# Linear attention and a SwiGLU block on one core: the statements from the eleventh chunk of tile 0 on in another order, some casts, multiplications and additions on another engine

## The chip, the core and the metric

The kernel runs on one core of a Trainium2 chip. A core has five engines with a queue each: TensorE (PE in the profile; its weight loads are PEld), VectorE (DVE), ScalarE (ACT), GpSimd (POOL) and SyncE (SP), which here issues nearly all transfers. An engine executes its queue in order; engines wait for each other by semaphores. 16 DMA engines move the data between device memory (HBM) and the on-chip memory, and one kind of transfer, the DMA transpose, also transposes. TensorE multiplies: it loads a block of weights, streams a second operand past it, and writes into one of eight accumulation banks. The metric is device time in microseconds (us) of one execution, the median of several.

## The reference: what is computed

Attention without softmax, with a decay `lam` for each head, in blocks of 64 positions, and a SwiGLU block on its result. q, k and v are 4 x 8 x 768 x 64 (batch, head, position, dimension), x is 3072 x 512, the weights are 512 x 1536 (two) and 1536 x 512.

```python
for b in range(nb):
    sl = slice(b * block, (b + 1) * block)
    qb, kb, vb = (q[:, :, sl].copy(), k[:, :, sl].copy(), v[:, :, sl].copy())
    intra = np.einsum('bhic,bhjc->bhij', qb, kb) * Dmask[None]
    intra = np.einsum('bhij,bhjd->bhid', intra, vb)
    inter = np.einsum('bhid,bhde->bhie', qb * lam_pow[None], kv_state)
    out[:, :, sl] = intra + inter
    ...
    kv_state = lam_block[None, :, None, None] * kv_state + np.einsum('bhsd,bhse->bhde', kb_dec, vb)
...
x = np.ascontiguousarray(attn_out.transpose(0, 2, 1, 3)).reshape(B * S, H * D)
g = x @ w_gate
silu = g * (1.0 / (1.0 + np.exp(-g)))
val = x @ w_val
return (silu * val @ w_out).astype(np.float32)
```

## The kernel before

The work is cut into twelve groups of the attention (256 positions of one batch element each, all heads) and six tiles of the SwiGLU block (512 tokens each, two groups). Group g feeds tile g // 2, so the attention of the next groups runs between the matmuls of the tile at hand. Everything is written out by hand: the kernel has a manual schedule, and each engine's queue holds its instructions in the order in which the statements stand. `use(...)` names the accumulation banks that the next statement takes.

For a group g the statements are:

- `load_fp32(g, ...)`: k, q and v from HBM, on SyncE's queue
- `kcast(g)` (ScalarE) and `qcast(g, engine)`: k rounded to bf16, q multiplied by its decay and rounded, both into the tile `qk`; `v_scale(g, engine)`: v times its decay, into `v_s`
- `dma_transpose(g)`: `qk` transposed into `qkt`, a DMA on SyncE's queue (L268), from group 3 on; groups 0 to 2 are transposed on TensorE
- `scores(g)`: k times q on TensorE (reads `qkt`); `mask(g, ...)`: the causal mask, on VectorE
- `upd_mm(g)`: this group's contribution to the state (reads `qk` and `v_s`); `sadd`, `kvn`, `kvm`, `kv0c`, `kvz`, `kvf0`: additions to the running state, its decay, and casts of it to bf16
- `op_new(g)` / `op_bare(g)`, `inter(g, first)`, `intra(g, first)`: the output, from the state (reads `qkt`) and from the masked scores; between the two stands `guard(g)`, a ScalarE copy of one column of the bank, for which the second of them waits
- `evr(g, r, engine)`: the output out of the bank, as the tile `xt` of the SwiGLU block

For a tile t: `ffn_gate(t, fc, b0, b1)` and `ffn_val(t, fc, b0, b1)` are 4 matmuls each for one chunk fc (128 of 1536 hidden features) and blocks b0 to b1 of the tile's tokens; the first ends in the SiLU on ScalarE (tile `sil`, four buffers), the second in the multiplication of `sil` by the bank on VectorE (into `h`). `ffn_out(t, b)` is the last product for 128 tokens of tile 0. Tiles 1 to 5 have their last product, and tiles 4 and 5 the first two as well, in a form with seven products of quarter size and sums of the operands (`hs_new`, `hsum`, `oprod`, `w_combo`, `x_combo`, `unit`, `uprod`, `silu`, `mu`, `mup`, `wo_combo`). The weights arrive in pieces (`w_piece`, `wo_piece`) and are rounded by `w_cast` and `wo_cast`. All loads but one pair at the start, the transposes and the stores but one stand in SyncE's queue. q, k, raw weights and several of the sums share ten buffers.

The lines that matter below: `inter(2, False)` L992, `evr(2, 0, DVEC)` L993, `kcast(3)` L996, `qcast(3, nc.gpsimd)` L997, `dma_transpose(3)` L998, the loads after it from L999 on, `v_scale(3, nc.gpsimd)` L1002, `dma_transpose(4)` L1019, `load_fp32(5, nc.sync, v, "v")` L1020, the six `wo_piece` from L1021 on, `scores(3)` L1035, `dma_transpose(5)` L1072, `inter(4)` L1098 and `upd_mm(5)` L1103, `ffn_out(0, 0)` L1119, `ffn_gate(2, 3, 0, 2)` L1122, `inter(5)` L1124, `scores(5)` L1125.

Of the kernel before, what the change touches and what calls it, by code (L numbers as in the profile page):

```python
# [37 lines left out]
def _body(ctx, tc, nc, q, k, v, lam, moe_w_gate, moe_w_val, moe_w_out, out):  # L38
# [896 lines left out]
    def use(*bk):  # L935
        fixed[:] = bk
# [72 lines left out]
    use(0); ffn_gate(1, 0, 0, 2)  # L1009
    use(1); ffn_val(1, 0, 0, 2)  # L1010
    use(2); ffn_gate(1, 1, 0, 2)
    use(3); ffn_val(1, 1, 0, 2)
    use(4); ffn_gate(1, 2, 0, 2)
    use(5); ffn_val(1, 2, 0, 2)
    use(6); ffn_gate(1, 3, 0, 2)
    use(7); ffn_val(1, 3, 0, 2)
    kcast(4)
    qcast(4, nc.vector)
    dma_transpose(4)  # L1019
# [7 lines left out]
    use(0); ffn_gate(1, 4, 0, 2)  # L1027
    use(1); ffn_val(1, 4, 0, 2)
    use(2); ffn_gate(1, 5, 0, 2)
    use(3); ffn_val(1, 5, 0, 2)  # L1030
    use(4); ffn_gate(1, 6, 0, 2)
    use(5); ffn_val(1, 6, 0, 2)
    use(6); ffn_gate(1, 7, 0, 2)
    use(7); ffn_val(1, 7, 0, 2)
    use(0, 1, 2, 3); scores(3)  # L1035
    use(4, 5); upd_mm(3)
    mask(3, 1, 0)
    mask(3, 0, 0)
    mask(3, 0, 1)
# [3 lines left out]
    use(7); ffn_val(1, 8, 0, 2)  # L1043
    mask(3, 1, 1)
    use(2); ffn_gate(1, 9, 0, 2)
    use(4); ffn_gate(1, 10, 0, 2)
    use(6); ffn_val(1, 9, 0, 2)
    use(0, 1); op_new(3)
    inter(3, True)
    use(2); ffn_val(1, 10, 0, 2)  # L1050
    guard(3)
    intra(3, False)
    use(3, 4); upd_mm(4)
    evr(3, 0, DVEC)
    kcast(5)
    evr(3, 1, ACTC)
    use(7); ffn_gate(1, 11, 0, 2)
    sadd(3, 1)
    sadd(4, 0)
    use(2); ffn_val(1, 11, 0, 2)  # L1060
    kvn(4, 0, ACTC)
    use(6); ffn_gate(1, 0, 2, 4)
    use(1); ffn_gate(1, 1, 2, 4)
    use(0); ffn_gate(1, 2, 2, 4)
    sadd(4, 1)
    qcast(5, nc.vector)
    use(5); ffn_gate(1, 3, 2, 4)
    use(2); ffn_val(1, 1, 2, 4)
    use(7); ffn_val(1, 2, 2, 4)
    use(6); ffn_val(1, 0, 2, 4)  # L1070
    use(1); ffn_gate(1, 4, 2, 4)
# [4 lines left out]
    use(3); ffn_gate(1, 5, 2, 4)  # L1076
    use(2, 0, 6, 4); scores(4)
    v_scale(5, nc.gpsimd)
    kvm(3, nc.gpsimd)
# [4 lines left out]
    mask(4, 0, 1)  # L1084
    mask(4, 1, 1)
    use(3); ffn_val(1, 3, 2, 4)
    mask(4, 1, 0)
    use(5); ffn_gate(1, 6, 2, 4)
    use(7); ffn_val(1, 4, 2, 4)
    use(4); ffn_gate(1, 7, 2, 4)  # L1090
    use(3); ffn_val(1, 5, 2, 4)
    use(1); ffn_gate(1, 8, 2, 4)
    use(7, 4); op_new(4)
    use(0); ffn_gate(1, 9, 2, 4)
    use(6); ffn_val(1, 9, 2, 4)
    mask(4, 0, 0)
    use(3); ffn_val(1, 6, 2, 4)
    inter(4, True)  # L1098
    guard(4)
    w_combo(0, 0, (0, 3))  # L1100
    use(6); ffn_val(1, 7, 2, 4)
    intra(4, False)
    use(3, 5); upd_mm(5)  # L1103
    evr(4, 1, ACTC)
    evr(4, 0, ACTC)
    new_xt(3)
    use(1); ffn_gate(1, 10, 2, 4)
    use(0); ffn_val(1, 8, 2, 4)
    use(4); ffn_gate(1, 11, 2, 4)
    use(7); ffn_gate(2, 0, 0, 2)  # L1110
    use(0); ffn_val(2, 0, 0, 2)
    wo_cast(ACTC)
    use(2); ffn_gate(2, 1, 0, 2)
    wo_combo(0)
    sadd(5, 0)
    use(1); ffn_val(1, 10, 2, 4)
    wo_cast()
    kvn(5, 0, ACTC)
    use(4); ffn_out(0, 0)  # L1119
    use(0); ffn_val(1, 11, 2, 4)  # L1120
    use(7); ffn_gate(2, 2, 0, 2)
    use(4); ffn_gate(2, 3, 0, 2)  # L1122
    use(1, 6); op_new(5)
    inter(5, True)  # L1124
    use(3, 2, 7, 0); scores(5)  # L1125
    kvm(4, nc.vector)
    mask(5, 1, 0)
    mask(5, 0, 0)
    mask(5, 0, 1)
    w_combo(1, 0, (0, 3))  # L1130
    sadd(5, 1)
    wo_combo(1)
    mask(5, 1, 1)
    guard(5)
    kcast(6)
    use(4); ffn_out(0, 1)
    qcast(6, nc.vector)
    dma_transpose(6)
# [4 lines left out]
    use(7); ffn_out(0, 2)  # L1143
    intra(5, False)
    evr(5, 0, ACTC)
    evr(5, 1, ACTC)
    hs_new(1)
    use(2); ffn_out(0, 3)
    hsum(1, 0, 0, 6, 0, 1)
    hsum(1, 0, 0, 6, 1, 2)  # L1150
    hsum(1, 1, 0, 6, 1, 2)
    wo_combo(2)
    hsum(1, 2, 0, 6, 0, 1)
    use(7); ffn_gate(2, 0, 2, 4)
    use(5); ffn_val(2, 1, 0, 2)
    use(0); ffn_val(2, 3, 0, 2)
    use(6); ffn_val(2, 2, 0, 2)
    use(4); ffn_val(2, 0, 2, 4)
    hsum(1, 1, 0, 6, 0, 1)
    use(5); ffn_gate(2, 1, 2, 4)  # L1160
    hsum(1, 2, 0, 6, 1, 2)
    wo_combo(3)
    v_scale(6, nc.vector)
    use(7); ffn_gate(2, 2, 2, 4)
    use(2); ffn_gate(2, 3, 2, 4)
    use(3); ffn_val(2, 2, 2, 4)
    hsum(1, 3, 0, 6, 0, 1)
    use(7); ffn_val(2, 1, 2, 4)
    use(0); ffn_gate(2, 4, 0, 4)
    use(5); ffn_val(2, 4, 0, 4)  # L1170
    use(1); ffn_gate(2, 5, 0, 4)
    kcast(7)
    use(3, 4); scores(6)
    use(6, 2); upd_mm(6)
    mask(6, 0, 1)
    use(7); ffn_val(2, 5, 0, 4)
    sadd(6, 0)
    kvm(5, nc.gpsimd)
    qcast(7, nc.gpsimd)
# [4 lines left out]
    out_new(1, (0,), [0, 1, 7], 0)  # L1184
    oprod(1, 0, 1)
    kvn(6, 0, ACTC)
    w_combo(0, 1, (0, 3))
    use(4); ffn_val(2, 3, 2, 4)
    sadd(6, 1)
    use(5); ffn_gate(2, 6, 0, 4)  # L1190
    oprod(1, 0, 7)
    oprod(1, 0, 2)
    kvn(6, 1, ACTC)
    v_scale(7, nc.vector)
    sadd(6, 2)
    mask(6, 0, 0)
    kv0c(3, ACTC)
    use(4); ffn_gate(2, 7, 0, 4)
    kvn(6, 2, ACTC)
    oprod(1, 0, 6)  # L1200
    sadd(6, 3)
    use(6); ffn_val(2, 6, 0, 4)
    hsum(1, 3, 0, 6, 1, 2)
    oprod(1, 0, 5)
    oprod(1, 0, 4)
    use(0); ffn_val(2, 7, 0, 4)
# [3 lines left out]
    use(3, 7); op_new(6)  # L1210
    inter(6, True)
    use(0, 4); upd_mm(7)
    use(2, 6); scores(7)
    kvm(6, nc.vector)
    sadd(7, 0)
    v_scale(8, nc.gpsimd, 0, 4)
    guard(6)
    kvn(7, 0, ACTC)
    mask(7, 0, 0)
    sadd(7, 1)  # L1220
    intra(6, False)
    evr(6, 1, ACTC)
    use(1); ffn_gate(2, 8, 0, 4)
    kvn(7, 1, ACTC)
    kcast(8)
    sadd(7, 2)
    mask(7, 0, 1)
    use(5); ffn_val(2, 8, 0, 4)
# [5 lines left out]
    out_new(1, (1,), [2, 1, 7], 0)  # L1234
    oprod(1, 1, 7)
    oprod(1, 1, 1)
    use(6); ffn_gate(2, 9, 0, 4)
    kvn(7, 2, ACTC)
    sadd(7, 3)
    oprod(1, 1, 6)  # L1240
    v_scale(8, nc.vector, 4, 8)
    w_combo(1, 1, (0, 3))
    use(0); ffn_gate(2, 10, 0, 4)
    evr(6, 0, ACTC)
    use(5); ffn_val(2, 10, 0, 4)
    use(6); ffn_val(2, 9, 0, 4)
    oprod(1, 1, 4)
    oprod(1, 1, 2)
    oprod(1, 1, 5)
    hs_new(2)  # L1250
    use(7, 3); op_new(7)
    inter(7, True)
# [431 lines left out]
```

## Time and profile before

| | |
|---|---|
| time, median of 3 | 216.13 us (216.01 to 216.83) |
| the profiled execution's own time | 215.75 us |
| its span, first to last instruction | 214.0 us |
| granted TensorE clock | 1.00 |
| TensorE busy | 207.5 us, 97% of the span, 2801 matmuls |
| VectorE, ScalarE, GpSimd busy | 157.5, 131.8, 50.9 us |
| moved by DMA | 39.77 MB, mean 186 GB/s |
| q, 512 KB a load, median from issue to landing | 7.5 us |
| w_out, 512 KB a piece, median from issue to landing | 9.1 us |
| DMA transpose, median from issue to landing | 3.9 us |

How to read it: the page is one profiled execution. Lines of a timeline give start and length in us, engine, line of the kernel, operation, output <- input, sizes, and how often; in brackets stands how long the engine was idle just before, and what ended that. The busy rows of the page cut the span into 40 slices of 5.35 us; each digit is a busy share in tenths. Matmuls overlap each other, so how far apart they start says more than how long each is; their ends are modelled. For SyncE (SPq) the length of a line is the time in which it issues the transfer, not that of the transfer. A transfer lands in 16 parts, one for each DMA engine, and the trace records each.

### The profile page before, as it was taken

The page shows a single profiled execution, that of the slowest core. Times are in us where ns is not written, and L with a number is a line of the kernel's source. Part 1 is how long each engine was busy: PE and PEld are TensorE (multiplying, and loading weights), DVE is VectorE, ACT ScalarE, POOL GpSimd, SP SyncE. Part 2 cuts the span into 40 slices and gives each one's busy share as a digit, 9 for nine tenths or more (in the row PEclk, how much of TensorE's full clock was granted, in tenths as well). Part 3 has the DMA queues.
Part 4 walks back from the last instruction along what each step waited for, and adds up shares of the span by engine and source line. Part 5 has one row for each costly group of instructions (what it writes and reads, how often), then busy time and mean ns, then how long its engine had stood idle before and what let it go on. Part 6 is the DMA issues. An engine that isn't in the chain of part 4 may idle for free.

```text
span 214.0 us, 6802 instructions
## 1 busy us (share of the span) xinstructions
PE 207.5 (97%) x2801; PEld 153.0 (72%) x2801; DVE 157.5 (74%) x302; ACT 131.8 (62%) x283; POOL 50.9 (24%) x72
## 2 busy tenths in 40 slices
PE   7799999999999999999999999999999999999993
PEld 3466455888886558767654545888888888888883
DVE  1673447679774798889779899999887589982851
ACT  6788576657446443667677385946873677536522
POOL 6585755704472010300101030040200000000200
PEclk9999999999999999999999999999999999999999
DMA  6999999999996697989677869776000500005014
GB/s 187 343 352 373 378 365 324 266 256 222 356 335 132 168 280 188 240 204 261 156 189 163 208 144 248 185 69 228 6 3 3 196 0 3 0 0 199 0 54 147
DMA packets 82177, 39.77 MB, mean 186 GB/s; under 512 B 45410, under 2 KB 77794, under 8 KB 82146
## 3 DMA queue, kind: packets, MB, share of 16 engines
q1 hardware_dynamic: 80946, 38.74, 66.7%
q10 hardware_dynamic: 1200, 0.59, 1.0%
q8 instruction: 22, 0.36, 0.7%
q14 instruction: 9, 0.07, 0.1%
HBM read 28.31 MB, written 6.29 MB: 162 GB/s over the span
## 4 chain that ended last, share of the span: by engine, by line
PE 92%; SPq 3%; DMA 2%; POOL 1%; issue 0%; ACT 0%; DVE 0%
PE bank L814 22%; PE bank L600 20%; PE bank L618 20%; PE bank L755 17%; PE bank L638 5%; SPq L109 2%; DMA v<-in_v_dram 2%; PE bank L541 2%; PE bank L554 2%; PE bank L408 1%; PE bank L347 1%; POOL v_s L260 1%; PE bank L383 1%; PE bank L310 0%; ACT kvf L501 0%
## 5 line engine op out<-in xcount | busy, mean ns | idle before, releaser
L622 DVE TENSOR_TENSOR h<-sil,bank 128x256 bf16<-128x256 bf16 (+1 forms) x67 | 35.0, 532 | 21.4 <-PE bank L618 17.2
L618 PE MATMUL bank<-xt,wv_sb 128*128 128x256 bf16 (+1 forms) x276 | 50.2, 314 | 0.0
L600 PE MATMUL bank<-xt,wg_sb 128*128 128x256 bf16 (+1 forms) x276 | 50.1, 315 | 0.0
L605 ACT ACTIVATE sil<-bank 128x256 bf16<-128x256 f32 (+1 forms) x67 | 31.6, 477 | 22.3 <-PE bank L600 15.7
L618 PEld LDWEIGHTS <-wv_sb 128*128 128x128 bf16 x276 | 26.6, 98 | 14.7
L600 PEld LDWEIGHTS <-wg_sb 128*128 128x128 bf16 x276 | 26.1, 98 | 12.9
L260 POOL TENSOR_TENSOR v_s<-v,dec 128x512 bf16<-128x512 f32 (+1 forms) x15 | 18.6, 1254 | 60.9 <-DMA v<-in_v_dram 19.8
L814 PEld LDWEIGHTS <-h 128*128 128x128 bf16 x240 | 23.5, 98 | 3.6
L814 PE MATMUL bank<-wo_sb,h 128*128 128x256 bf16 x180 | 22.3, 273 | 0.0
L814 PEld LDWEIGHTS <-hs 128*128 128x128 bf16 x180 | 17.5, 98 | 3.4 <-DVE hs L673 0.2
L362 DVE TENSOR_TENSOR ssb<-bank,causal 128x512 bf16<-128x512 f32 x24 | 15.5, 684 | 3.6 <-PE bank L347 3.5
L814 PE MATMUL bank<-wt,hs 128*128 128x256 bf16 x120 | 15.6, 272 | 0.0
L755 PEld LDWEIGHTS <-ws 128*128 128x128 bf16 x144 | 14.0, 98 | 1.8
L755 PE MATMUL bank<-xs,ws 128*128 128x256 bf16 x96 | 13.9, 272 | 0.0
L763 DVE TENSOR_TENSOR bank<-bank,es 128x512 f32<-128x512 f32 x12 | 8.3, 697 | 7.2 <-PE bank L755 4.4
L780 DVE TENSOR_TENSOR h<-sil,bank 128x512 bf16<-128x512 bf16 x18 | 11.8, 679 | 1.5 <-ACT sil L774 1.2
L780 POOL TENSOR_TENSOR h<-sil,es 128x512 bf16<-128x512 bf16 x1 | 1.2, 1162 | 46.7 <-DVE es L765 46.7
L774 ACT ACTIVATE sil<-bank 128x512 bf16<-128x512 f32 x18 | 10.2, 593 | 2.1 <-PE bank L755 2.1
L638 PE MATMUL bank<-wo_sb,h 128*128 128x512 bf16 x48 | 10.9, 379 | 0.0
L755 PE MATMUL bank<-xt,wv_sb 128*128 128x256 bf16 x72 | 10.8, 273 | 0.0
L443 ACT CAST kvn<-kvf 64x256 bf16<-64x256 f32 x22 | 8.9, 403 | 3.1 <-DVE kvf L489 2.7
L278 ACT CAST qk<-kraw 128x1024 bf16<-128x1024 f32 x9 | 9.4, 1042 | 1.8 <-DMA kraw<-in_k_dram 1.8
(127 smaller groups left out, 342.9 us busy)
## 6 DMA issues: line engine op xcount, KB each, us to landing
out_dram<-osb SPq DMA_DIRECT2D x22, 256.0 KB, 2.7
v<-in_v_dram SPq DMA_DIRECT2D x18, 256.0 KB, 4.3
woraw<-in_moe_w_out_dram SPq DMA_DIRECT2D x6, 512.0 KB, 9.1
kraw<-in_k_dram SPq DMA_DIRECT2D x24, 128.0 KB, 3.2
qraw<-in_q_dram SPq DMA_DIRECT2D x24, 128.0 KB, 3.8
wraw<-in_moe_w_gate_dram SPq DMA_DIRECT2D x5, 512.0 KB, 6.9
wraw<-in_moe_w_val_dram SPq DMA_DIRECT2D x5, 512.0 KB, 6.7
kraw<-in_k_dram SPq DMA_DIRECT2D x4, 512.0 KB, 6.3
```

Source lines behind the costliest of these rows:

```text
L260: eng.tensor_tensor(out=st[("vs", g)][:, h0:h1], in0=st[("v", g)][:, h0:h1].rearrange("p h (s d) -> p h s d", s=2), in1=vfac(g, h0, h1), o ...
L278: fn(out=qk_new(g)[:, 0].rearrange("p s (h d) -> p h s d", h=H), in_=st[("kraw", g)].rearrange("p h (s d) -> p h s d", s=2))
L362: nc.vector.tensor_tensor(out=st[("ssb", g)][:, h2, 2 * c:2 * c + 2].rearrange("p a s n -> p a (s n)"), in0=st[("sp", g, c, h2)].rearrange ...
L600: nc.tensor.matmul(gp[:, n0:n1], wg_sb[:, mc, fs], xt[:, g0:g1, mc].rearrange("p g b n -> p g (b n)"), start=(mc == 0 and n0 == 0), stop=( ...
L605: nc.scalar.activation(sil[:, 0:N], gp[:, 0:N], AF.Silu)
L618: nc.tensor.matmul(vp[:, n0:n1], wv_sb[:, mc, fs], xt[:, g0:g1, mc].rearrange("p g b n -> p g (b n)"), start=(mc == 0 and n0 == 0), stop=( ...
L622: nc.vector.tensor_tensor(out=h_sb[:, fc % FH, b0:b1].rearrange("p b n -> p (b n)"), in0=sil[:, 0:N], in1=vp[:, 0:N], op=ALU.mult)
L638: nc.tensor.matmul(ps, st[("h", t, fc // FH)][:, fc % FH, b], wo_sb[:, fc, c0:c1], start=(fc == 0), stop=(fc == FC - 1))
L755: nc.tensor.matmul(o[i][:, fi * 256:fi * 256 + 256], lhs(c, 2 * j + fi), rhs(c), start=(k < 2 and fi == 0 and c == 0), stop=(c == KH - 1), ...
L774: nc.scalar.activation(sil[half, r], unit_src(t, j, half, r)[0], AF.Silu)
L780: eng.tensor_tensor(out=st[("h", t, half)][:, 2 * j:2 * j + 2][:, :, r:B:2], in0=v3(st[("u", t, j)][4][half, r]), in1=v3(unit_src(t, j, ha ...
L814: nc.tensor.matmul(o, lhs(f), rhs(f), start=(k in (1, 7) and f == 0), stop=(f == FH - 1), skip_group_check=True)
```

## The change

Up to chunk 9 of tile 0 (counted from 0) and `scores(2)` the kernels are equal. From there to the end the same statements, with the same shapes, stand in another order, and many take other accumulation banks. The functions are unchanged; no work is added or left out. The order on SyncE's queue is the same.

On another engine stand: `v_scale(3)` and `qcast(3)` (GpSimd before, VectorE after), `kvm(3)` and `kvm(5)` (GpSimd, then VectorE), `kv0c(2)` (GpSimd, then ScalarE), the second half of `v_scale(8)` (VectorE, then GpSimd), `mup(4, 0)` (VectorE, then GpSimd) and `evr(10, 1)` (VectorE, then ScalarE). The one-line pieces of `hsum`, `mask`, `sadd`, `kvn`, `silu` and `mu` move with the rest.

The beginning of the diff, with all that concerns groups 2 and 3:

```diff
     use(2, 3, 4, 5); scores(2)
+    use(6); ffn_gate(0, 10, 0, 4)
     mask(2, 0, 0)
+    mask(2, 1, 0)
     mask(2, 0, 1)
-    mask(2, 1, 0)
     mask(2, 1, 1)
-    use(6); ffn_gate(0, 10, 0, 4)
-    use(7); ffn_val(0, 10, 0, 4)
     use(0); ffn_gate(0, 11, 0, 2)
-    use(1); ffn_val(0, 11, 0, 2)
-    use(2, 3); upd_mm(2)
+    use(2); ffn_gate(0, 11, 2, 4)
+    use(1); ffn_val(0, 10, 0, 4)
+    use(7, 2); upd_mm(2)
+    use(6, 0); op_bare(2)
+    intra(2, True)
+    kcast(3, ACTC)
     kvz(2)
-    kvf0(2)
-    use(4, 5); op_bare(2)
-    intra(2, True)
     guard(2)
     inter(2, False)
     evr(2, 0, DVEC)
+    use(4); ffn_val(0, 11, 2, 4)
+    use(6); ffn_val(0, 11, 0, 2)
+    v_scale(3, nc.vector)
+    qcast(3, nc.vector)
     evr(2, 1, ACTC)
-    sadd(2, 1)
-    kcast(3)
-    qcast(3, nc.gpsimd)
+    use(3); ffn_gate(1, 0, 0, 2)
+    use(1); ffn_gate(1, 1, 0, 2)
     dma_transpose(3)
     load_fp32(4, nc.sync, v, "v")
-    use(6); ffn_gate(0, 11, 2, 4)
-    use(7); ffn_val(0, 11, 2, 4)
-    v_scale(3, nc.gpsimd)
-    v_scale(4, nc.gpsimd)
-    kvm(2, nc.gpsimd)
-    kv0c(2, POOLC)
     load_fp32(5, nc.sync, k, "kraw")
     load_fp32(5, nc.sync, q, "qraw")
...
+    use(2); ffn_gate(1, 7, 0, 2)
+    use(7, 1, 0, 3); scores(3)
...
+    use(0, 3); op_new(4)
+    inter(4, True)
+    use(6, 7); upd_mm(5)
+    guard(4)
+    intra(4, False)
...
+    use(3); ffn_gate(2, 1, 0, 2)
+    use(4); ffn_gate(2, 2, 0, 2)
+    use(1); ffn_out(0, 0)
+    kv0c(2, ACTC)
+    use(5, 0); op_new(5)
+    use(2, 6, 4, 3); scores(5)
+    inter(5, True)
...
+    use(2); ffn_val(2, 2, 0, 2)
     qcast(6, nc.vector)
+    use(3); ffn_gate(2, 3, 0, 2)
```

In the new order `ffn_val(1, 7, 0, 2)` stands after `scores(3)` and `upd_mm(4)`, and `ffn_gate(2, 3, 0, 2)` after `scores(5)` and `inter(5)`; both stood ahead of them before.

More of the change, by code (lines that the diff above doesn't have):

```diff
@@ L1075, in _body @@
     load_fp32(6, nc.sync, v, "v")
[L1076 to L1079, printed above, removed]
+    mask(4, 1, 1)
+    mask(4, 1, 0)
+    use(3); ffn_gate(1, 8, 2, 4)
+    use(1); ffn_val(1, 4, 2, 4)
+    use(5); ffn_val(1, 8, 2, 4)
+    use(4); ffn_val(1, 6, 2, 4)
+    use(0, 3); op_new(4)
[3 more added lines that the diff above has]
+    intra(4, False)
+    w_combo(0, 0, (0, 3))
+    new_xt(3)
+    evr(4, 0, ACTC)
+    use(1); ffn_gate(1, 9, 2, 4)
+    evr(4, 1, ACTC)
+    use(5); ffn_gate(1, 10, 2, 4)
+    use(4); ffn_val(1, 7, 2, 4)
+    use(0); ffn_val(1, 10, 2, 4)
+    use(2); ffn_gate(1, 11, 2, 4)
     wo_cast()
@@ L1209, in _body @@
     store(1, 0, 0, 0, 512, None)
-    use(3, 7); op_new(6)
+    use(5, 6); op_new(6)
     inter(6, True)
-    use(0, 4); upd_mm(7)
-    use(2, 6); scores(7)
-    kvm(6, nc.vector)
+    use(4, 1); upd_mm(7)
+    use(0, 3); scores(7)
     sadd(7, 0)
-    v_scale(8, nc.gpsimd, 0, 4)
     guard(6)
     kvn(7, 0, ACTC)
-    mask(7, 0, 0)
[L1220 to L1224, printed above, removed]
+    intra(6, False)
+    sadd(7, 1)
+    v_scale(8, nc.gpsimd, 0, 4)
+    kvn(7, 1, ACTC)
+    kv0c(4, ACTC)
+    use(7); ffn_gate(2, 8, 0, 4)
+    use(2); ffn_gate(2, 9, 0, 4)
+    kv0c(3, ACTC)
+    v_scale(8, nc.gpsimd, 4, 8)
+    mask(7, 0, 1)
+    mask(7, 0, 0)
+    kvm(6, nc.vector)
+    sadd(7, 2)
     kcast(8)
-    sadd(7, 2)
-    mask(7, 0, 1)
-    use(5); ffn_val(2, 8, 0, 4)
+    w_combo(1, 1, (0, 3))
     qcast(8, nc.vector)
@@ L1418, in _body @@
     uprod(4, 0, 6, 0)
-    silu(4, 0, 1, 0)
-    use(3, 5); op_new(10)
-    hs_new(4)
+    use(2, 3); upd_mm(11)
     inter(10, True)
-    use(7, 0); upd_mm(11)
     uprod(4, 0, 6, 1)
     sadd(11, 0)
+    silu(4, 0, 1, 1)
+    silu(4, 0, 1, 0)
     silu(4, 0, 0, 1)
```

690 lines of the change are left out of this document (332 added, 358 removed).

## The prediction

> **What bounds the kernel now.** I read the page first: the busy shares, then the slices.
>
> ```profile
> span 214.0 us, 6802 instructions
> ...
> PE 207.5 (97%) x2801; PEld 153.0 (72%) x2801; DVE 157.5 (74%) x302; ACT 131.8 (62%) x283; POOL 50.9 (24%) x72
> ...
> PE   7799999999999999999999999999999999999993
> ...
> PEclk9999999999999999999999999999999999999999
> DMA  6999999999996697989677869776000500005014
> ```
>
> PE is busy throughout but for the first two slices and the last, at full clock, and DMA is saturated in the first third. A busy PE can hide waits, so I looked at how far apart matmuls start: 109 ns for 256 columns and 216 ns for 512, almost everywhere after 16 us. What is lost there is small: 0.49 us at 38.1 us (inter(2) after the guard), and after 70 us five gaps of 0.05 to 0.11 us, 0.41 us in all. Each change of tile size costs 0.093 us going into a group of 64x64 matmuls and about 0.12 us coming out. So reordering has little to win, about 1 us, and can only lose by making PE wait for something that comes late. Therefore I looked for what PE waits for already: the weight loads, then SyncE's queue.
>
> ```profile
> 70.29 0.11 PEld L541 LDWEIGHTS <-kv 64*64 64x64 bf16 x2 [0.21 <-DMA qkt<-qk]
> ```
>
> This is inter(5), at its first weight load: PE gets there in the same tenth of a microsecond as the transposed k and q of group 5. It is the only place after 16 us where PE depends on a transfer with no margin. The queue that brings it:
>
> ```profile
> 36.08 1.35 SPq L109 DMA_DIRECT2D qraw<-in_q_dram  x1
> 40.73 2.33 SPq L268 DMA_TRANSPOSE qkt<-qk  x1
> 43.11 0.57 SPq L109 DMA_DIRECT2D v<-in_v_dram  x1
> 43.72 0.58 SPq L109 DMA_DIRECT2D kraw<-in_k_dram  x1
> 44.34 1.46 SPq L109 DMA_DIRECT2D qraw<-in_q_dram  x1
> 45.97 5.44 SPq L268 DMA_TRANSPOSE qkt<-qk  x1
> 51.45 0.58 SPq L109 DMA_DIRECT2D v<-in_v_dram  x1
> 52.09 3.89 SPq L249 DMA_DIRECT2D woraw<-in_moe_w_out_dram  x6
> 56.14 10.39 SPq L268 DMA_TRANSPOSE qkt<-qk  x1
> 66.58 3.51 SPq L124 DMA_DIRECT2D kraw<-in_k_dram  x4
> ```
>
> The transposes are those of groups 3, 4 and 5 (start, then length). SyncE holds its queue while it issues one (2.33, 5.44, 10.39 us: the later two until what is ahead has nearly landed). From 36.08 to 40.73 it waits for the casts that the first transpose reads; after that nothing pauses for over a microsecond until 66.5, and the DMA share of the stretches is 0.8 to 1.3 (0.45 in 41 to 42 us). What is late at 40.73 is late at 70.17, where the last of the 16 parts of transpose 5 lands.
>
> **The change, part by part.** SyncE's instructions stand in the same order in both programs. What decides when transpose 3 starts is this:
>
> ```profile
> 39.60 1.04 ACT L278 CAST qk<-kraw 128x1024 bf16<-128x1024 f32 x1
> 37.73 1.91 POOL L282 TENSOR_TENSOR qk<-qraw,dec 128x1024 bf16<-128x1024 f32 x1 [1.70 <-DVE ssb L362]
> 39.60 1.91 POOL L260 TENSOR_TENSOR v_s<-v,dec 128x1024 bf16<-128x1024 f32 x1
> 38.44 0.73 DVE L569 CAST xt<-bank 128x512 bf16<-128x512 f32 x1
> ```
>
> Before: qcast(3) ends on GpSimd at 39.64, kcast(3) on ScalarE at 40.64; the transpose starts 0.09 later, at 40.73.
>
> After, step 1: kcast(3) moves ahead of guard(2) and ends by about 38 us, but qcast(3) goes to VectorE, whose queue is then evr(2,0), the two multiplications of ffn_val(0,11), v_scale(3), qcast(3). inter(2) is followed by the two ffn_val, 4 matmuls of 109 ns each: 38.91 + 0.44 = 39.35 for the second, whose result is there 0.60 later (that row's length), at 39.95. Its multiplication takes 0.42: 40.4. v_scale(3) and qcast(3) take 1.22 each on VectorE (rows L260 and L282 there: 1216 ns), with 0.08 of overlap: 41.5 and 42.6. Its v landed at 39.06, so it does not wait. Transpose 3 starts at 42.6 + 0.09 = 42.7: 1.97 late. GpSimd, which did this multiplication in 1.91 from 37.73, stands idle then. The multiplications of ffn_val(1,0) and others queue behind the two long ones.
>
> Step 2, how much arrives at 70 us. All of it: +1.97. Least: issuing takes 2.10 (the median of the nine transposes) instead of 2.33, -0.23; and the last part of transpose 5 came 1.58 after the other fifteen (68.44 to 68.59), because a 16 KB instruction fetch held one DMA engine for 1.12 us from 67.85. Without that, 1.97 - 0.23 - 1.58 = +0.16. PE's fetches come by its instruction count, which the new order reaches within 0.6 us of the same time; the transpose is then still waiting or moving, so I keep one fetch of 1.12: 1.97 - 0.23 - 1.58 + 1.12 = +1.28. I take +1.3: it lands at 71.5.
>
> The Trainium skill (DMA: Bandwidth & Descriptors, "Queues, rings and completion order") says that each DMA engine takes turns between queue rows by packet, so fetch and data share an engine. By that rule alone a fetch ahead of the transpose delays it like one inside it, and the sum would be that of +1.3; if it finds the engine idle it costs nothing, which is the lower end.
>
> Step 3, when PE gets there. In the new order gate (2,3) comes after scores(5) and inter(5), 4 x 109 = 0.44, and inter(4), upd_mm(5), intra(4) stand together, one change of tile size less: 0.093 + 0.122 = 0.22. Unhindered, PE reaches scores(5) at 70.29 - 0.66 = 69.6. Two small waits come before: scores(3), now at 46.4 (46.88 less ffn_val(1,7), 0.44), needs transpose 3, which lands 3.7 to 4.3 after its start (group 3 now 4.3), 46.4 to 47.0: 0 to 0.6; ffn_out(0,0) needs the last w_out piece, 66.66 + 1.75 and a cast of 1.04, 69.45, against 67.0 + 10 x 0.216 = 69.2: 0.3. Neither adds to the end, because the wait at scores(5) takes them in: PE arrives near 70.2 and waits 1.4. If scores(5) did not wait, they would cost their 0.3 to 0.9. The guard wait of 38.1 stays: scores, update, intra, guard, inter keep their order.
>
> Step 4, the rest. After scores(5) PE has the work it had, plus gate (2,3): +0.44. Of the 0.41 of small gaps I count half as gone, -0.2 (0 and -0.41 are the ends). The other moves cost nothing on the path: kvm(3), kvm(5) to VectorE, 0.42 each; half of v_scale(8), 0.76, and one multiplication of tile 4, 0.68, to GpSimd (1.09 and 1.16 there); evr(10,1), 0.72, to ScalarE; kv0c(2), 0.40, to ScalarE. With v_scale(3) and qcast(3), VectorE gets 1.1 us more on 157.5, hidden under PE; uncovered it would be those 1.1 us.
>
> Sum: 1.3 + 0.44 - 0.2 = +1.54. The profiled execution took 215.75 (its span 214.04 and 1.71 around it): 217.3; the median, 216.13, lies 0.38 higher: **217.7 us**.
>
> **Rivals.**
> - *The delay is mostly absorbed.* The DMA engines stand idle for about 0.55, 0.34 and 0.21 us at 41, 44 to 46 and 53 us; later transfers might close these, or the fetch falls elsewhere. For it: fifteen parts landed at 68.6. Against: the idle moments follow the transposes, which stay. With +0.16 to +0.8: 216.5 to 217.2.
> - *Not slower: the transfers have room.* If transpose 5 lands before PE's 69.6, PE never waits there, and only the order counts: -0.22 and -0.2 to -0.4, 215.5 to 215.7. The point from which it decides is 69.6, 0.6 earlier than now, with its start 2 us later. Against it stands the 0.21 above. A gain over 1.08 would need every gap of before gone.
> - *The clock falls during the wait.* At half clock, as at the start, where 512 columns take 426 ns and not 216, 3.4 us of work cost 1.7 more: 219.4. No row shows so long a wait; the longest at full clock was 0.91, without effect. The Trainium skill (TensorE: Matmul & The Clock Gate, "What's actually happening") has the clock drop after an idle window of about 3.4 us, above the 1.4 here, so I give it little.
>
> **How the numbers follow.** Forecast (the delay reaches scores(5), +0.9 to +2.0): 217.2 to 218.6, 0.66. Absorbed: 0.19. Not slower: 0.11. Clock: 0.03. Something unseen: 0.01. The range leaves out the clock and most of "not slower": 216.3 to 218.6; its top is +1.97 + 0.44 = +2.41. A measurement here tells 0.5% from no change, 1.08 us: slower means over 217.21, all of the forecast and the clock, 0.69; same takes in the absorbed case and most of "not slower", 0.28; faster 0.03.
>
> **What would show it.** SyncE starts its third-group transpose near 42.7 and the fifth's parts land near 71.5; at scores(5) the weight loads show 1 to 1.8 us of idle time released by the DMA of qkt; before it waits at scores(3) and at ffn_out(0,0) of under 0.6; after it PE without gaps. Wrong if the transpose starts by 41, if PE meets scores(5) without a wait, or if a new gap over 0.5 us comes after 75 us.

## The result: 0.26% slower, and the profile after

The changed kernel takes 216.65 us (median of 22 runs, 216.27 to 217.50) against 216.03 us for the kernel before on the same chip (22 runs, 215.70 to 217.12). The ratio is 1.0026, with a 95% interval of 1.0015 to 1.0037: slower by 0.6 us, less than half of the 1.6 us that were forecast. The profiled execution after took 216.91 us, its span 215.2 us (215.75 and 214.0 before): by chance the two profiled executions lie 0.26 us above and 0.28 us under their medians, so their difference, 1.16 us, is nearly twice that of the medians.

The page of the kernel after, its head and three of its slice rows:

```profile
span 215.2 us, 6790 instructions
...
PE 207.6 (96%) x2797; PEld 153.7 (71%) x2801; DVE 159.0 (74%) x303; ACT 132.7 (62%) x285; POOL 48.4 (23%) x69
...
PE   8889999999999999999999999999999999999993
...
PEclk9999999999999999999999999999999999999998
DMA  6999999879999797999685859854000500005014
```

TensorE's work and clock are unchanged, VectorE has 1.5 us more and GpSimd 2.5 us less. The page can't show 0.6 us; the loss is found by following the steps of the prediction. VectorE's queue at the start of the change, kernel after:

```profile
40.53 1.23 DVE L260 TENSOR_TENSOR v_s<-v,dec 128x1024 bf16<-128x1024 f32 x1 [0.15 <-DMA v<-in_v_dram]
41.67 1.22 DVE L282 TENSOR_TENSOR qk<-qraw,dec 128x1024 bf16<-128x1024 f32 x1
```

SyncE's queue of the same run (a line is start, length of the issue, transfer):

```profile
36.62 1.35 SPq L109 DMA_DIRECT2D qraw<-in_q_dram  x1
43.05 1.75 SPq L268 DMA_TRANSPOSE qkt<-qk  x1
44.86 0.57 SPq L109 DMA_DIRECT2D v<-in_v_dram  x1
45.53 0.65 SPq L109 DMA_DIRECT2D kraw<-in_k_dram  x1
46.23 1.29 SPq L109 DMA_DIRECT2D qraw<-in_q_dram  x1
47.69 5.78 SPq L268 DMA_TRANSPOSE qkt<-qk  x1
53.51 0.59 SPq L109 DMA_DIRECT2D v<-in_v_dram  x1
54.20 4.24 SPq L249 DMA_DIRECT2D woraw<-in_moe_w_out_dram  x6
58.60 8.39 SPq L268 DMA_TRANSPOSE qkt<-qk  x1
67.04 3.50 SPq L124 DMA_DIRECT2D kraw<-in_k_dram  x4
```

qcast(3) stands behind v_scale(3), which here had to wait 0.15 us for its v, and ends at 42.9; transpose 3 starts at 43.05 instead of 40.73. The delay goes down the queue: +2.3, +1.7, +2.5 us at the starts of transposes 3, 4 and 5. What TensorE has of it, its weight loads of the kernel after:

```profile
46.94 0.48 PEld L347 LDWEIGHTS <-qkt 64*64 64x64 bf16 x32 [0.75 <-DMA qkt<-qk]
...
51.85 0.33 PEld L408 LDWEIGHTS <-qk 64*64 64x64 bf16 x31 [0.38 <-issue]
...
70.70 0.48 PEld L347 LDWEIGHTS <-qkt 64*64 64x64 bf16 x32 [0.42 <-DMA qkt<-qk]
```

The idle time in brackets has to be read against the same place in a kernel that does not wait: at scores(3) it is 0.21 us there, at scores(5) 0.42 us (rows below). So TensorE stands 0.75 - 0.21 = 0.54 us at scores(3), for transpose 3, and 0.4 us at upd_mm(4): that one waits for v_scale(4), which on GpSimd starts when the late v(4) has landed (49.75):

```profile
49.88 1.91 POOL L260 TENSOR_TENSOR v_s<-v,dec 128x1024 bf16<-128x1024 f32 x1 [3.64 <-DMA v<-in_v_dram]
```

At scores(5), where the forecast had 1.4 us, it does not stand at all. From the starts of successive matmuls: 0.54 at scores(3), 0.44 at upd_mm(4), 0.15 at the guard of group 4, 1.13 us together.

The ledger of the two profiled executions: TensorE begins scores(5) 0.41 us later than it began inter(5) before (70.70 and 70.29), still has gate (2,3) to do, 0.44, and loses 0.16 less in small gaps and changes of tile size later (what remains of the difference): its last matmul starts 0.69 us later (211.24, before 210.55). From there to the end of the span it takes 3.96 us instead of 3.49: another 0.47. 0.69 + 0.47 = 1.16. The second term was in no step of the forecast, and the page does not show it: nothing but semaphore instructions runs there.

### The profile page after: what moved, and what is told of

Same layout as the page of the kernel before. It is cut to its first block, busy times and chain, and to the rows that moved or that the text cites. A ratio compares the mean times of both kernels' runs of the same rounds, so it can differ in the third digit from the quotient of the medians.

```text
span 215.2 us, 6790 instructions
## 1 busy us (share of the span) xinstructions
PE 207.6 (96%) x2797; PEld 153.7 (71%) x2801; DVE 159.0 (74%) x303; ACT 132.7 (62%) x285; POOL 48.4 (23%) x69
## 4 chain that ended last, share of the span: by engine, by line
PE 86%; DMA 5%; DVE 2%; ACT 2%; issue 1%; POOL 1%; SPq 1%; DVEq 0%; POOLq 0%; ACTq 0%
PE bank L814 21%; PE bank L755 17%; PE bank L618 16%; PE bank L600 16%; DMA v<-in_v_dram 5%; PE bank L638 5%; PE bank L554 2%; PE bank L541 2%; PE bank L408 1%; DVE ssb L362 1%; PE bank L310 1%; POOL v_s L260 1%; PE bank L383 1%; PE bank L182 1%; PE bank L148 1%
## 5 line engine op out<-in xcount | busy, mean ns | idle before, releaser
L618 PE MATMUL bank<-xt,wv_sb 128*128 128x256 bf16 (+1 forms) x276 | 49.2, 314 | 0.0
L600 PE MATMUL bank<-xt,wg_sb 128*128 128x256 bf16 (+1 forms) x276 | 48.8, 315 | 0.0
L780 POOL TENSOR_TENSOR h<-sil,es 128x512 bf16<-128x512 bf16 x2 | 2.3, 1162 | 55.4 <-ACT sil L774 48.1
L827 ACT COPY osb<-bank 128x256 f32<-128x256 f32 x10 | 3.7, 372 | 12.9 <-PE bank L814 12.9
```

The lines of the kernel that those rows point to most:

```text
L600: nc.tensor.matmul(gp[:, n0:n1], wg_sb[:, mc, fs], xt[:, g0:g1, mc].rearrange("p g b n -> p g (b n)"), start=(mc == 0 and n0 == 0), stop=( ...
L618: nc.tensor.matmul(vp[:, n0:n1], wv_sb[:, mc, fs], xt[:, g0:g1, mc].rearrange("p g b n -> p g (b n)"), start=(mc == 0 and n0 == 0), stop=( ...
L780: eng.tensor_tensor(out=st[("h", t, half)][:, 2 * j:2 * j + 2][:, :, r:B:2], in0=v3(st[("u", t, j)][4][half, r]), in1=v3(unit_src(t, j, ha ...
```

## Experiments

Ratios are to the kernel before on the same chip, with the 95% interval. "Start of T3" is SyncE's start of transpose 3, "T5 landed" the time at which the last of the 16 parts of transpose 5 landed. The theories: T, the loss is the late transpose 3, paid where TensorE first needs what comes late; R1, it lies elsewhere in the new order; R2, transpose 5 lands when it lands, so time won before it is lost again at scores(5); later E and S, on the end. Where an expectation counts runs, the first, second and third are those of the cast on GpSimd, of the cast first, and of both on GpSimd.

### Is it the late transpose?

The unchanged kernel after a second time:

> The kernel after, unchanged, beside the others on one chip, to see which of its rows come back. Theory T (its loss is the late transpose 3): waits of about 0.5 us at scores(3) and 0.4 at upd_mm(4) again, transpose 5 landing near 70.5, 216.5 to 216.8. If the early landing of transpose 5 was chance, it lands anywhere from 70.2 to 72 and a wait appears at scores(5). The second theory E (the end): in the profile after, a fetch of 8 KB of instructions falls at 213.31, behind the last matmul, where before has it at 208.28, and the span ends 1.45 us behind the last landing instead of 0.98; expected again: 1.3 to 1.5.

216.53 us, 1.0023 (1.0009 to 1.0037). The waits come back, 0.29 us at scores(3) and 0.40 us at upd_mm(4), and none at scores(5); T5 landed at 69.49, a microsecond earlier than in the first profile. The last part of the expectation, on the end, holds too: 1.44 us.

Cast back on GpSimd:

```diff
     v_scale(3, nc.vector)
-    qcast(3, nc.vector)
+    qcast(3, nc.gpsimd)
```

> The kernel after, with the cast of group 3's queries and keys (qcast(3)) back on GpSimd, where it waits neither for v(3) nor for the scaling on VectorE. Theory T (the whole loss is the late transpose 3 and what follows it, paid at scores(3), 0.54 us, and at upd_mm(4), 0.44 us): transpose 3 starts at about 40 to 41 instead of 43.05, both waits go, and the time is 216.65 - 0.54 - 0.44 = about 215.7. Rival R1 (the loss lies elsewhere in the new order): transpose 3 starts as early, the time stays 216.65 within 0.2. Rival R2 (transpose 5 lands no earlier than about 70.2 whatever its start, so TensorE, coming 0.9 us earlier, stands at scores(5) instead): both waits go and one of 0.4 to 0.9 us stands at scores(5); 216.1 to 216.5.

216.18 us, 1.0001 (0.9981 to 1.0020). T3 starts at 41.16, both waits are gone and none appears at scores(5). The loss is undone, though no more than that: not the 215.7 of T. The end is shorter here too, 1.21 us instead of 1.45, because SyncE has two instructions fewer (last table below); the next run, with an end of 1.45, is the one that changes the transpose alone.

Cast on VectorE, but first:

```diff
+    qcast(3, nc.vector)
     v_scale(3, nc.vector)
-    qcast(3, nc.vector)
```

> The kernel after, with qcast(3) still on VectorE but ahead of v_scale(3) instead of behind it. T: transpose 3 starts about 1.2 us earlier, at 41.8; the waits at scores(3) and upd_mm(4) shrink by up to 0.54 and 0.44 us: 215.7 to 216.0. R1: 216.65 within 0.2. R2: 216.1 to 216.5, with a wait at scores(5).

216.06 us, 1.0007 (0.9987 to 1.0027). T3 starts at 41.73. The weight loads of this kernel at scores(3) and scores(5), the rows that show no wait:

```profile
46.46 0.48 PEld L347 LDWEIGHTS <-qkt 64*64 64x64 bf16 x32 [0.21 <-issue]
...
69.79 0.48 PEld L347 LDWEIGHTS <-qkt 64*64 64x64 bf16 x32 [0.42 <-issue]
```

So the engine of the cast does not matter; that it stood behind a multiplication which nobody needed so early does.

Both on GpSimd, the cast first:

```diff
-    v_scale(3, nc.vector)
-    qcast(3, nc.vector)
+    qcast(3, nc.gpsimd)
+    v_scale(3, nc.gpsimd)
```

> The kernel after, with qcast(3) and v_scale(3) both on GpSimd, the cast first: VectorE is also rid of 2.4 us. T: transpose 3 at about 40 to 41 and 215.7, as with the cast alone, since VectorE is not what TensorE waits for after 43 us. R1: 216.65 within 0.2. If VectorE's two operations delay something else on TensorE, this run is faster than the cast alone, by up to 0.3 us.

216.02 us, 0.9987 (0.9965 to 1.0008). T3 starts at 40.05, no waits, an end of 1.28 us; freeing VectorE of 2.4 us shows no gain that could be told from the run before.

The cast still later on VectorE, behind the multiplication of ffn_val(1, 0):

```diff
-    qcast(3, nc.vector)
     evr(2, 1, ACTC)
...
+    new_xt(2)
+    use(4); ffn_gate(1, 2, 0, 2)
+    use(0); ffn_val(1, 0, 0, 2)
+    qcast(3, nc.vector)
     dma_transpose(3)
```

> The kernel after, with qcast(3) still on VectorE but behind the multiplication of ffn_val(1, 0, 0, 2) too, so that transpose 3 and the three loads behind it start about 1.4 us later again (44.5). T with direct payment: the wait at scores(3) grows from 0.54 by 1.2 to 1.5 us, TensorE comes later to everything behind by that much, and the time is 217.8 to 218.2. If the queue has room before scores(3) after all: 216.6 to 217.2. If transpose 5 binds as the prediction had it, a wait at scores(5) comes on top: over 218.2.

217.01 us, 1.0053 (1.0033 to 1.0073). T3 starts at 43.48, only 0.4 to 0.7 us later than after, not 1.4. TensorE's weight loads of this kernel at scores(3):

```profile
47.41 0.48 PEld L347 LDWEIGHTS <-qkt 64*64 64x64 bf16 x32 [1.23 <-DMA qkt<-qk]
```

1.23 - 0.21 = 1.02 us at scores(3), nothing at upd_mm(4), which TensorE now reaches later, and nothing at scores(5). The delay is paid at scores(3), one for one: transpose 3 landed at 47.37 against 46.64 in the repeat, +0.73, and the wait there is 1.02 against 0.29, +0.73. With the 0.40 at upd_mm(4) that the repeat had, the waits grow by 0.33 in all, the time on the same chip by 0.48.

The same delay in the old order, the kernel before with both on VectorE:

```diff
-    qcast(3, nc.gpsimd)
+    v_scale(3, nc.vector)
+    qcast(3, nc.vector)
     dma_transpose(3)
...
-    v_scale(3, nc.gpsimd)
```

> The kernel before, with v_scale(3) and qcast(3) on VectorE one behind the other, at the place where qcast(3) stood on GpSimd. Transpose 3 starts about 1.1 us later than before, at 41.8. T: the delay alone costs in the old order what the chain of transfers lets through, 0 to 1.1 us: 216.0 to 217.1, and if the whole difference between the kernels before and after is this delay, about 216.4 to 216.7. R1 (the delay costs nothing; the order does): 216.0 within 0.2.

216.17 us, 1.0001 (0.9983 to 1.0018). T3 starts at 42.93, about as late as after, and yet there is no wait at scores(3):

```profile
47.18 0.48 PEld L347 LDWEIGHTS <-qkt 64*64 64x64 bf16 x32 [0.21 <-issue]
```

It landed at 46.80, and in the five profiles of the old order TensorE comes at 46.9 to 47.2. In the new order it would come to scores(3) at 46.4 to 46.9 without waits, 0.5 us earlier in the mean, ffn_val(1, 7) having moved behind it. It takes both parts of the change to make the wait: the later cast and the earlier scores.

### Where transpose 5 lands

From the profiles of all kernels of some 216 us, sorted by the start of transpose 5 (derived from the trace; us). "Issue ends" is when SyncE has issued it, "w_out" when the last of the six pieces of w_out ahead of it has landed:

```
kernel                          T5 starts   issue ends    w_out   15 parts landed   last part landed
before                            56.14       66.53       66.66        68.59             70.17
before, 16 stores split           56.47       66.95       67.09        69.04             70.57
both on GpSimd, stores split      56.78       66.27       66.39        68.33             69.90
both on GpSimd                    56.90       66.11       66.25        68.19             69.73
before, longer end                57.00       65.59       65.72        67.66             69.21
cast first, nine memsets (256 B)  57.36       66.27       66.40        69.70             69.75
cast first                        57.37       65.39       65.54        68.85             68.89
both on GpSimd, guard covered     57.74       66.86       66.98        70.50             70.52
cast first, stores split          57.90       65.50       65.63        68.94             68.96
cast on GpSimd                    57.94       65.59       65.72        69.07             69.08
after, repeated                   58.07       65.98       66.11        69.48             69.49
after, stores split               58.33       65.95       66.08        69.38             69.41
before, both on VectorE           58.41       66.29       66.42        69.76             69.80
before, 12 stores split           58.55       67.58       67.78        69.55             69.56
after                             58.60       67.00       67.14        70.45             70.47
after, cast still later           58.71       67.56       67.70        69.60             69.67
```

The delay hardly travels. From the first five rows to the four with the order after (after, its repeat, its stores split, cast still later) the start of transpose 5 moves by 1.77 us in the mean (56.66 to 58.43), the end of its issue by 0.33 (66.29 to 66.62), and its last part lands 0.16 earlier (69.92 to 69.76). It is the same within the old order: with both on VectorE transpose 5 starts 2.3 us later than in the kernel before, and its issue ends 0.2 us earlier. Whenever SyncE begins with it, its issue ends 0.12 to 0.19 us before the last piece of w_out has landed. In the kernel before, one DMA engine was behind with these pieces: of the fifth one, fifteen parts had landed by 62.77 and the sixteenth came at 65.37; after, it was 65.78 and 65.87. So the transfers had room for more than 2 us there. The stretch from 63 to 66.5 us shows it, before and after (its length; busy time of PE, PEld, DVE, ACT and POOL; granted clock, DMA share, GB/s):

```profile
63.00:66.50 3.50, 3.50 (x65) 3.04 (x50) 2.13 (x5) 3.28 (x7) 1.04 (x1) 1.00 1.26 88
```

```profile
63.00:66.50 3.50, 3.50 (x51) 3.07 (x40) 1.75 (x3) 2.63 (x6) 3.13 (x4) 1.00 1.28 341
```

From the end of the issue to the last part it takes 3.45 to 3.67 us in fourteen rows and 1.97 to 2.10 in two (before, 12 stores split; after, cast still later). In the fourteen a 16 KB fetch of TensorE's instructions reaches into that time, in the two it is over before the issue ends. In the first five rows one part alone is late, 1.53 to 1.58 us behind the other fifteen, in the other nine all sixteen are. For scores(5), which needs the last part, this makes little difference: 3.64 us before, 3.47 after. In all sixteen kernels it lands between 68.89 and 70.57, whatever T3's start (40.0 to 43.5).

### The end of the program

The first guess was that a fetch of 8 KB of instructions which fell at 213.31 after and at 208.28 before made the end longer, and that it was VectorE's, whose queue has nine instructions fewer in the new order:

```diff
     nc.vector.memset(ones, 1.0)
+    nine = const.tile([128, 1], FP32, name="nine")
+    for _ in range(9):
+        nc.vector.memset(nine, 0.0)
```

(on the kernel with the cast first).

> The kernel after with qcast(3) ahead of v_scale(3), as in the second run, and nine memsets of one column on VectorE at the start, which nothing reads: VectorE then has as many instructions as before the change (the new order has nine fewer). Theory E: the fetch of 8 KB at the end belongs to VectorE's instructions and lay at 208.28 before because of their number; with the nine it comes back to about 208, the span ends about 1.0 us behind the last landing instead of 1.45, and the time falls from 216.06 to about 215.6. Rival: the fetch is another engine's or falls by chance; then the end stays 1.2 to 1.45 us and the time 216.0 to 216.2.

226.61 us, 1.0498 (1.0470 to 1.0525): something else became 10 us slower (the last part of this section). For the question asked: the fetch moved to 218.07, 2.4 us ahead of the last matmul, as before the change (2.3), and the end stayed 1.45 us. So the fetch is VectorE's, and it is not the cause. The guess is refuted.

What the trace then showed: SyncE's instructions at the end are waits for the last stores, then closing drains, and one of them is held. It is always the one with the same number from the start, the 208th in the trace. In `before` SyncE has only 207. Another 8 KB fetch goes with it: in every kernel one starts 1.0 to 1.3 us behind the end of the 207th instruction, at 215.02 after, and at 199.66 in the kernel after with twelve stores split (below), where the 207th ends at 198.38.

Four stores of the kernel before split in two, so that there are five more instructions on SyncE:

```diff
-        (eng or (nc.sync if t >= SY else nc.scalar)).dma_start(
+        for c0, c1 in (((c0, (c0 + c1) // 2), ((c0 + c1) // 2, c1)) if t in (4,) else ((c0, c1),)):
+            (eng or (nc.sync if t >= SY else nc.scalar)).dma_start(
```

> The kernel before, with only the four output stores of tile 4 split in two, so that SyncE has five more instructions, about as many as after. S: the held instruction falls among the closing drains, the end grows from 0.98 to about 1.45 us and the time by 0.4 to 0.5, to 216.5. Rival: the end stays 1.0 us and the time 216.0 to 216.1.

216.35 us, 1.0012 (0.9998 to 1.0026), and an end of 1.43 us. The end is as expected; the time lies at the lower side, and its interval does not exclude no change.

Twelve stores of the kernel after split (the same edit with `t in (2, 3, 4)`):

> The kernel after, with the twelve output stores of tiles 2, 3 and 4 each split into two halves by columns, so that SyncE has 19 more instructions; nothing else. Theory S (the end): in all profiles so far one instruction of SyncE, always the one with the same number from the start, is held 0.35 to 0.4 us; before it lies past the end, after, with four more semaphore instructions on SyncE, it is the first of the closing drains, and the span ends 1.45 us behind the last landing instead of 0.98. With 19 more the held one is an output store or a wait long before the end: the end falls back to about 1.0 us and the time by 0.4 to 0.5, to 216.1. Rival (the end's length has another cause): 1.45 us and 216.5 stay.

215.99 us, 0.9998 (0.9982 to 1.0014): the loss is gone, although TensorE still stands 0.34 us at scores(3) (0.55 idle there instead of 0.21). The end is 0.95 us.

The control, the same twelve stores split in the kernel before:

> The kernel before with the same twelve output stores split as in the runs with the split: the control for them. The held instruction of SyncE lies past the end before the change, so by theory S nothing is to be won: 216.0 within 0.2, an end of about 1.0 us. Rival: the split itself is worth time (smaller stores land sooner), and the gain of the split in the order after was that: 215.5 to 215.7.

216.59 us, 1.0034 (1.0022 to 1.0046), a miss: slower. With 223 instructions the 208th falls among the last four stores. It started 0.379 us behind the one before it, and the last landing came 2.76 us behind the last matmul instead of 2.51. No clean control, then; with sixteen split (`t in (1, 2, 3, 4)`) it lies 6.6 us before the last matmul:

> The kernel before with the sixteen output stores of tiles 1 to 4 split: as many instructions on SyncE as in the runs of the new order with the split, so that the held instruction lies some 12 us before the end and not among the last four stores as with twelve stores split (there it delayed a store by 0.33 us and the last landing by 0.25). Theory S, and the split itself costs nothing: end 0.95 us, last landing 2.5 us behind the last matmul's start, 216.0 within 0.2. If the split itself costs or gains time on the kernel before: 216.3 and more, or under 215.8.

215.95 us, 0.9998 (0.9978 to 1.0017). Splitting stores is worth nothing by itself. The profiles side by side (derived from the trace):

```
                             SyncE's        the 208th:                last matmul's start  last landing to
kernel                     instructions     which one, and pause     to last landing, us  end of span, us
before                         207          -                              2.51               0.98
before, 4 stores split         212          1st drain, 0.375               2.51               1.43
before, both on VectorE        210          wait behind 2nd drain, 0.395   2.52               1.04
before, 12 stores split        223          wait of a last store, 0.379    2.76               0.95
before, 16 stores split        228          a store, not back to back      2.59               0.97
after                          211          2nd drain, 0.372               2.51               1.45
after, repeated                211          2nd drain, 0.371               2.53               1.44
cast on GpSimd                 209          3rd drain, 0.402               2.51               1.21
both on GpSimd                 209          3rd drain, 0.402               2.52               1.28
cast first                     211          2nd drain, 0.390               2.51               1.45
after, 12 stores split         230          a store, 0.371                 2.50               0.95
```

The pause is from the end of the instruction before it to its start; between the first two drains of the kernel before it is 0.057 us. A drain that is held itself takes 116 to 136 ns instead of 7. What it costs depends on which one it is: 0.45 to 0.47 us at the first or second drain, 0.2 to 0.3 at the third, 0.06 at the semaphore wait behind the second, in the kernel before with both on VectorE. What moved it into the end: with its new waits the order after has four more semaphore instructions on SyncE (68 against 64), with the same transfers.

### Both remedies, and one more

Casts on GpSimd and twelve stores split:

> The same split, and qcast(3) and v_scale(3) both on GpSimd, the cast first, as in the third run. If the waits (T) and the end (S) are the two parts of the loss and add up: the third run's end of 1.28 us falls to 1.0, so 0.3 under its 216.02: 215.7, faster than before by about 0.4. If S is wrong: 216.0.

215.77 us, 0.9989 (0.9970 to 1.0008), not told from the kernel before. An end of 0.96 us, no waits at scores(3) and upd_mm(4), and a new one at scores(5):

```profile
69.94 0.56 PEld L347 LDWEIGHTS <-qkt 64*64 64x64 bf16 x32 [0.63 <-DMA qkt<-qk]
```

0.63 - 0.42 = 0.21 us: TensorE now comes before transpose 5 has landed, at 69.90 here.

Cast first on VectorE, and the stores split:

> The order after with both remedies: qcast(3) ahead of v_scale(3) on VectorE (the second run, 216.06, end 1.45 us) and the twelve stores split (end 1.0 us). If the two parts of the loss add up: 216.06 - 0.45 = 215.6, faster than before by 0.4. If TensorE, coming earlier, stands at scores(5) for transpose 5 instead (0.2 us in the run with the casts on GpSimd): 215.8.

215.80 us, 0.9996 (0.9977 to 1.0015). No wait at any of the three places, an end of 0.95 us. The two remedies do not add up to the 1.0 us that their parts are worth in the profiles (0.55 and 0.47, see the last part of the next section): each alone, and both together, bring the time to that of the kernel before, within 0.2%.

Last, the guard wait of 0.5 us at 38.1, covered by moving four matmuls into it, on the kernel with the casts on GpSimd and the stores split ("the run before this one" in its expectation):

```diff
     guard(2)
+    use(4); ffn_val(0, 11, 2, 4)
     inter(2, False)
     evr(2, 0, DVEC)
-    use(4); ffn_val(0, 11, 2, 4)
     use(6); ffn_val(0, 11, 0, 2)
```

> As the run before this one, with ffn_val(0, 11, 2, 4) (0.44 us) between intra(2) and inter(2), where TensorE stands 0.5 us for the guard copy. The wait goes, two changes of tile size (0.093 + 0.122 us) come: 0.3 us less, 215.4. If scores(3) then waits for transpose 3, or a later wait takes it, 215.7.

217.03 us, 1.0034 (1.0018 to 1.0051): slower. Four of its twelve executions, the profiled one among them (216.26), took 216.2 to 216.5 us, the other eight 216.9 to 217.2; why is open. TensorE in the profiled one:

```profile
38.69 0.41 PE L541 MATMUL bank<-qkt,kvn 64*64 64x128 bf16 x8
39.98 0.60 PE L618 MATMUL bank<-xt,wv_sb 128*128 128x256 bf16 x4 [0.88 <-DVE xt L569]
```

Those matmuls had covered the next wait: ffn_val(0, 11, 0, 2) writes bank 6, which evr(2, 0) first has to empty. Covered at 38.1, the stall stands 0.9 us long at 39.1.

### The 10 us of nine memsets

The cover was first tried on the kernel with the memsets of one column:

> The run before this one with ffn_val(0, 11, 2, 4) (four matmuls of 109 ns, 0.44 us) moved between intra(2) and inter(2), where TensorE stands 0.5 us for the guard copy. The wait of 0.50 to 0.74 us goes, the matmuls pay 0.093 + 0.122 us for the two changes of tile size, so 0.3 us less: 215.3 if theory E holds, 215.75 if not. If something behind it waits instead (scores(3) on transpose 3, which the cast does not bring forward), the gain is eaten there.

227.91 us, 1.0529 (1.0489 to 1.0568), with the same move of the wait on top of the 10 us. What those come from is in SyncE's queue: the first lines are the kernel with the cast first and the nine memsets,

```profile
9.28 0.83 SPq L238 DMA_DIRECT2D wraw<-in_moe_w_gate_dram  x1
10.16 0.84 SPq L238 DMA_DIRECT2D wraw<-in_moe_w_val_dram  x1
```

and these the same kernel with a scratch tile of 256 instead of 32 bytes:

```profile
8.73 0.69 SPq L238 DMA_DIRECT2D wraw<-in_moe_w_gate_dram  x1
9.46 0.69 SPq L238 DMA_DIRECT2D wraw<-in_moe_w_val_dram  x1
```

The scratch tile moves the tiles behind it in the on-chip memory by its size. With 64 bytes (`[128, 16]`, written whole):

> As the run with nine memsets on VectorE that took 226.6 us, but their scratch tile has 16 columns of fp32 (64 bytes of a partition) instead of one, which took 32 bytes there and moved every later tile to an address that is an odd multiple of 32 bytes. Here the later tiles stay at multiples of 64. If the addresses cost the 10 us: loads are issued in 0.69 us each again instead of 0.83, and the time is 216.1, or 0.1 more for nine larger memsets. If the memsets or VectorE's number of instructions cost them: about 226.

226.61 us, 1.0481 (1.0451 to 1.0511); a miss, 64 is not enough. With 256 bytes (`[128, 64]`, one column written):

> As the run with the scratch tile of 64 bytes (226.61 us), with a tile of 256 bytes, of which the nine memsets write one column: the later tiles move by 256 bytes and lie at multiples of 256 again, as in the kernels of 216 us. If the addresses cost the 10 us and 256 bytes is what counts: 216.1 and loads issued in 0.69 us each. If it is the memsets or VectorE's number of instructions, or a larger multiple counts: 226.

216.46 us, 1.0008 (0.9986 to 1.0029). The addresses made it, not the memsets.

## Why the prediction was wrong

- **Step 1 was right.** Transpose 3 at 42.7 was forecast, 43.05 measured. Of the difference 0.15 is VectorE's wait for v(3), whose last part landed at 40.50 and not at 39.06; the repeat, without that wait, has 42.81.
- **Step 2 failed**, "I take +1.3: it lands at 71.5". It landed 0.30 later (70.47), and 0.68 earlier in the repeat. The failing term is the first, "1.97 - 0.23": that what is late at the start of transpose 3 is late by as much when transpose 5 moves. SyncE came to transpose 5 at 58.60 instead of 56.14, 2.5 us later, but its issue ended at 67.00 instead of 66.53: before, it stood behind the last w_out pieces, for which one DMA engine was late, and that time took in the rest. 0.47 stands where 1.74 was forecast. The other part, "- 1.58 + 1.12", -0.46 for the fetch, was -0.17 (3.47 us from the end of the issue to the last part instead of 3.64). 0.47 - 0.17 = 0.30. The text's lower bound, +0.16, is near that by luck: it keeps the whole delay and leaves out a fetch that was there.
- **Step 3 fell with it.** The "1.4" at scores(5) was nothing, so the small waits were paid directly, as the text had it for that case. Without waits TensorE was to come at 69.63; with the 1.13 of the three waits that makes 70.76, and 70.70 was measured. scores(3) cost 0.54, inside its "0 to 0.6"; ffn_out(0, 0) showed no wait of 0.3; upd_mm(4), 0.44, was not named: v(4) is the very next transfer behind transpose 3, and v_scale(4) on GpSimd waits for it. The order of transfers was followed only as far as the next transposes. The 0.21 at inter(5) was no wait either: the same 0.21 stands at scores(3) where nothing is late (46.46 and 47.18 above), and transpose 5 had landed 0.12 earlier.
- **Step 4 was right in size.** +0.44 for gate (2,3), and -0.16 for the small gaps against -0.2.
- **A term was missing**, the end: +0.47 in the profiles. Put into the kernel before it lengthened the end by 0.45 us (1.0012, an interval that does not exclude no change); taken out of the kernel after it shortened the end by 0.50 (1.0023 to 0.9998).
- **The sum.** 0.41 + 0.44 - 0.16 + 0.47 = 1.16 on the profiled executions, against 1.54. Of the medians, 0.62 us remain.

Of the rivals, "the delay is mostly absorbed" gave the right time (216.5 to 217.2), and for transpose 5 it is what happened, though at 63 to 66 us and not at the idle moments that it names. The time is right in part by luck: the delay is paid at scores(3) and upd_mm(4) instead, and the end comes on top. The clock stayed at 0.997.

How the 0.6 us divide is not settled. The start of the last matmul is 211.08 in the mean of three profiles with the late cast (after, repeat, stores split) and 210.53 in that of six with the early one, 0.55 us less; the end is 0.47. Together 1.0, so the rest of the new order should win some 0.4. But profiles of the old order vary by 1.2 us in the same measure (210.55 to 211.78), and the intervals of the ratios, about 0.2% to each side, do not separate 0.5 from 0.3.

## What to carry to other kernels

A transfer that comes late hurts at its first reader, and so do the ones right behind it in its queue: go through all of them in order before looking at the place where the margin is smallest. How late it makes a transfer further down is another question: look for what that one waits for last, and whether there is idle time ahead of it. When two edits are each harmless, an earlier consumer and a later producer, the wait may need both. And the time from the last matmul to the end is part of the time: compare it between two kernels, instruction by instruction, semaphores included.

## What was unexpected of the hardware

- One instruction of SyncE, the 208th in the trace, starts 0.37 to 0.40 us behind the one before it in every kernel in which the two stand back to back, whatever it is (drain, semaphore wait, store). Among the closing drains it costs 0.06 to 0.47 us, among the last four stores it made the last landing 0.25 us later, and at stores well before them it costs nothing. An 8 KB fetch of instructions starts 1.0 to 1.3 us behind the end of the 207th in all nineteen profiles, also where the 208th comes only 5 us later. So a boundary between blocks of instructions stands there, as far as the trace can tell; why passing it takes 0.4 us is not shown. The Trainium skill (Runtime: NRT & Kernel Launch, "Instruction fetch mechanics") calls the cost of such a boundary mostly hidden; this one is not hidden at the end.
- In this kernel tiles moved by 32 or 64 bytes off a multiple of 256 made loads slower: the issue of a weight load takes 0.83 us instead of 0.69, a load of 512 KB lands 8.3 us (32 bytes) or 7.9 us (64 bytes) after its issue instead of 6.9 (medians of the weights' gate loads), and the kernel takes 226.6 us instead of 216.1. Moved by 256 bytes they cost nothing; 128 was not tried. The Trainium skill (DMA: Bandwidth & Descriptors, "How a descriptor splits into AXI transactions") says that transfers are cut at multiples of 256 bytes and that one which starts off them costs extra, in bytes fetched unused and in some cases in a transaction more. It words this for reads, and here the tiles are written; that the rule is the cause is likely and not shown.
- Transpose 5 takes 1.97 to 2.10 us from the end of its issue to its last part where no fetch of TensorE's instructions reached into that time (two kernels), and 3.45 to 3.67 where one did (fourteen), though in five of these only one part of sixteen was late. That the fetch is the cause is likely and not shown: at transpose 4 of the kernel with the cast first a fetch fell into the transfer (at 53.62), and it took 2.0 us all the same.
